# Gated recurrence and two MLPs on one core: attention of two blocks ahead of the first MLP, the two blocks taken in turns

## The chip, the cores and the metric

The kernel runs on one core of a Trainium2 chip. The metric is the device time of one launch in microseconds (us), lower being better. Three timed runs of the kernel before gave 1014.69, 1015.67 and 1017.27 us (median 1015.67); one more execution was taken with the hardware profiler and gave 1016.47 us.

## The reference

Three stages, one after the other. The first is a linear recurrence with a state of 48 x 48 for each of 4 batches and 8 heads over 768 steps; its output is laid out as 3072 tokens of 384 features. Then a SiLU MLP (384 to 2048 to 384) and a gated SiLU MLP (384 to 1536 to 384). All in float32.

```python
for t in range(S):                                   # B, H, S, D = 4, 8, 768, 48
    state = alpha[:, :, t, :, None] * state + np.einsum('bhd,bhe->bhde', k[:, :, t], v[:, :, t])
    y[:, :, t] = np.einsum('bhd,bhde->bhe', q[:, :, t], state)
x = y.transpose(0, 2, 1, 3).reshape(B * S, H * D)
h = x @ moe_w_in;  x1 = (h * sigmoid(h)) @ moe_w_out
g = x1 @ moe2_w_gate
out = ((g * sigmoid(g)) * (x1 @ moe2_w_val)) @ moe2_w_out
```

## The kernel before, in words

The recurrence is done in 24 chunks of 128 steps (6 per batch; chunk `n` is position `n // 4` of batch `n % 4`). A chunk has four head pairs, numbered `g = 4n + p`; two pairs make a duo `d`. For a duo, VectorE scans the decays (`stage_a1`, `stage_a3`), GpSimd multiplies k and q by them (`kq`, `stage_a2`, `stage_a3`). For a pair, TensorE forms the scores `s` (`qkt`), VectorE masks them into `pt` (`causal`), and ScalarE copies the transposed keys `kt` out of the same score tile (`keys`). For a chunk, TensorE then forms the output `y`, the state increment `ds` and, from chunk 4 on, the part of the old state (`pv`); `chunk_end` copies `y` into `x` (rounded on ScalarE, the remainder by a subtraction on VectorE) and updates the state. Head pair 0 of a chunk has to be spread over the unused rows of `x`: in the first block by extra matmuls (`spread`, `v3`), in later blocks by six DMAs from `y3` at the end of the block.

Matrix products are in float32 split into a rounded high part and a remainder, three matmuls for one. The scores of the chunks of the first block (`n < NE`) are plain float32 matmuls; later scores are split, which needs `stage_b` (ScalarE) and `stage_c` (VectorE, GpSimd) for each duo.

The first MLP takes the chunks in seven blocks of 4, 3, 3, 3, 3, 4 and 4 chunks; a step is one feature tile `f` of 16: `g1` (hidden `h`, nine matmuls), SiLU twice on ScalarE (`gh`, `gf`), a subtraction on VectorE (`gl`), `g2` (nine matmuls into three accumulators `x1`). While block `j` goes through its 32 half-steps (`slot`), the attention of block `j + 1` is issued pair by pair within 24 of them. The weights arrive as 64-bit words in 32 units (two for each feature); each unit takes three operations on VectorE (`decode_unit`, L47, L52, L57), one on ScalarE (`high_unit`) and one on GpSimd (`low_unit`); `units1` moves each of these stages one unit on. All 32 units are decoded while block 0 is in the MLP. The results of the first MLP go to DRAM, and the second MLP follows, in six blocks.

Each engine takes its instructions in program order, as this code emits them (a manual schedule): what stands ahead in an engine's queue holds up what stands behind. Loads go through SyncE's queue, which is in order as well; a chunk's input `in` has two buffers.

Of the kernel before, what the change touches and what calls it, by code (L numbers as in the profile page):

```python
# [20 lines left out]
DM = H * D  # L21
# [199 lines left out]
def fast(ctx, tc, pk, w1, w2, out, bad_i):  # L221
# [16 lines left out]
    wp = ctx.enter_context(tc.tile_pool(name="wp", bufs=2 * NF1))  # L238
    ps = ctx.enter_context(tc.tile_pool(name="ps", bufs=1, space=PSUM))
    mp = ctx.enter_context(tc.tile_pool(name="mp", bufs=2))  # L240

    def bank(i, name):
        return ps.tile([128, 512], F32, tag=f"b{i}", name=name)

# [25 lines left out]

    start = mp.tile([128, 6 * 512], F32, tag="big", name="start", bufs=3)
# [4 lines left out]
    in_t, v_t, r_t = {}, {}, {}  # L276
# [5 lines left out]
    def load_in(n):  # L282
        if n >= NCH:
            return
        t = ap.tile([128, A_W + 2 * W], F32, tag="in", name=f"in{n}")
        in_t[n] = t[:, :A_W], t[:, A_W:].rearrange("p (x r t) -> p x r t", x=2, r=NP)
        if n:
            SP.dma_start(out=t, in_=pk[n, :, :A_W + 2 * W])
            return
        for i in range(2):  # L290
            for lo, w in ((0, 2 * CA), (A_W, W // 2), (A_W + W, W // 2)):
                one = 0 if lo else 1
                cs = slice(lo + i * (w + one), lo + (i + 1) * w + one)
                SP.dma_start(out=t[:, cs], in_=pk[n, :, cs])

    def load_v(n):
# [86 lines left out]
    def qkt(g):  # L383

        d, i = divmod(g, 2)
        n, p = divmod(g, NP)
        kf, qf = kq_t[d][:, 0, i], kq_t[d][:, 1, i]
        if n < NE:

            b = [bank(k, f"s{g}_{k}") for k in ((0, 1), (5, 4))[g % 2]]  # L390
            for h in range(2):
                r = slice(64 * h, 64 * h + 64)
                PE.matmul(b[h][:, :C], kf[r], qf[r], start=True, stop=True)
            PE.matmul(b[0][:, C:C + 2 * D], kf, columns(ident), start=True, stop=True)
            s_t[g] = [x[:, :C] for x in b], b[0][:, C:C + 2 * D]
# [7 lines left out]
        s_t[g] = [b[:, :2 * C].rearrange("p (h t) -> p h t", h=2)], b[:, 2 * C:]  # L403

    def causal(g):
        if g < NE * NP and g % NP == 0:
            pt = p0[g // NP % 2]
        else:
            pt = ap.tile([128, 2, C], F32, tag="pt", name=f"pt{g}", bufs=NP + 1)
        pt_t[g] = pt  # L410
        s = s_t[g][0]
        if len(s) == 1:
            DVE.tensor_tensor(
                out=pt, in0=s[0],
                in1=mask.rearrange("p (o t) -> p o t", o=1).to_broadcast([128, 2, C]), op=ALU.mult,
            )
        else:
            for h in range(2):
                DVE.tensor_tensor(out=pt[:, h], in0=s[h], in1=mask, op=ALU.mult)

# [9 lines left out]
    def pv(n):  # L430
# [4 lines left out]
        v = v_t[n]  # L435
        early = n % 2 if n < NE else 0
        y = y_t[n] = bank((6, 2)[early], f"y{n}")
# [45 lines left out]
    def chunk_end(n):  # L483
# [3 lines left out]
        if i == 0:  # L487
            x_t[j] = mp.tile([128, 2, KT, 512], F32R, tag="big", name=f"x{j}", bufs=3)
            if j:
                y3_t[j] = mp.tile([128, 2, 512], F32R, tag="y3", name=f"y3_{j}", bufs=1)  # L490
# [77 lines left out]

    def g1(j, f, lo=0, hi=None):
        w = len(blocks1[j]) * C  # L570
        if (j, f) not in h_t:

            h_t[j, f] = bank(f % 2 + (6 if j == 0 and f < 2 else 0), f"h{j}_{f}")[:, :w]
        xk = [(x_t[j][:, 0, k, lo:hi or w], x_t[j][:, 1, k, lo:hi or w]) for k in range(KT)]
        product(h_t[j, f][:, lo:hi or w], unit_t["1", 2 * f], xk)

# [15 lines left out]
    def g2(j, f):  # L592
        w = len(blocks1[j]) * C
        if f == 0:
            x1_t[j] = [bank(2 + m, f"x1_{j}_{m}")[:, :w] for m in range(KT)]
        u = unit_t["1", 2 * f + 1]
        gh, gl = act_t.pop((j, f))
        for m in range(KT):
            PE.matmul(x1_t[j][m], part(u, m), gh, start=(f == 0), stop=False)  # L599
            PE.matmul(x1_t[j][m], part(u, m, 1), gh, start=False, stop=False)  # L600
        for m in range(KT):
            PE.matmul(x1_t[j][m], part(u, m), gl, start=False, stop=(f == NF1 - 1))  # L602
        if f == NF1 - 1:
            t0 = blocks1[j][0] * C
            ev = mp.tile([128, KT, 512], F32, tag="big", name=f"x1e{j}", bufs=3)
# [91 lines left out]
    def attn(lag=1, more=True, first=None):  # L697
# [9 lines left out]
        if new is not None:  # L707
            d, odd = divmod(new, 2)
            early = new < NE * NP
            ahead = d + (2 if early else 3)  # L710
            if early and new and not odd:
                up_to("a1", ahead, stage_a1, ND)
            causal(new)
            keys(new)
            if new == 0:
                up_to("a1", ahead, stage_a1, ND)
        if rest:
# [3 lines left out]
        if new is None:  # L721
            return
        if early and new % NP == 0:
            spread(new // NP)
        if odd:
            up_to("a3", ahead, stage_a3, ND)
            if not early:
                up_to("b", d + 2, stage_b, ND)
            up_to("gd", d, guard, ND)
        else:  # L730
            up_to("a1", ahead, stage_a1, ND)
            if not early:
                up_to("c", d + 1, stage_c, ND)
            up_to("a2", ahead, stage_a2, ND)

    late = []

    def load1(u):
# [3 lines left out]
        else:  # L742
            if u == NU1 - 4:
                late.append(mp.tile([128, 4, 2 * DM], I32, tag="big", name="late", bufs=3))
            load_unit(("1", u), w1_src(u), late[0][:, u - NU1 + 4])
# [34 lines left out]

    load_in(0)
    load_v(0)
    load_in(1)
    load_v(1)
# [23 lines left out]

    T0, BG, CG, TF, TE = 7, 2, 1, 1, 1

    first = NE * NP
    st["b"] = st["c"] = NE * NP // 2
    stage_a(0)
    stage_a(1)
    up_to("l1", 1, load1, NU1)
    for i in range(NP):
        ACT.activation(
            out=qh[:, i, 2 * C:].rearrange("p (h d) -> p h d", h=2), in_=columns(ident), func=AF.Copy
        )
    for g in range(first):  # L820
        attn(2)
        if g % 4 == 3:
            up_to("l1", g // 2 + 1, load1, NU1)
        if g >= T0:
            units1(0, 1 + (g - T0) // 2)
        if g == first - BG:
            up_to("b", first // 2, stage_b)
        if g == first - CG:
            up_to("c", first // 2, stage_c)

    for f in range(2):
        need1(2 * f)
        g1(0, f, 0, (NE - 1) * C)
        attn(1, False)
        for _ in range(TF):
            units1(8)
    up_to("b", first // 2 + 1, stage_b)
    stage_a(first // 2 + 2)
    for _ in range(TE):
        units1(8)  # L840

# [31 lines left out]

    steps = [(j, f) for j in range(NB1) for f in range(NF1)]
    def slot(j, hs, first=None):
        if j + 1 < NB1:
            done = sum(len(bl) for bl in blocks1[:j + 1]) * NP
            todo = len(blocks1[j + 1]) * NP
            due = sum(24 * m // todo <= hs for m in range(todo))
            attn(more=st["qk"] < done + due, first=first)  # L880
        else:
            attn(more=False, first=first)
        if j == 0:
            units1()

        if j == NB1 - 2 and hs == 26:
# [14 lines left out]

    g1(*steps[0], (NE - 1) * C)
    act1(*steps[0])()
    for s, (j, f) in enumerate(steps):
        need1(2 * f + 1)
        if s + 1 < len(steps):
            need1(2 * steps[s + 1][1])
            g1(*steps[s + 1], 0 if s else (NE - 1) * C)
        slot(j, 2 * f, (lambda: act1(*steps[s + 1])) if s + 1 < len(steps) else None)
        g2(j, f)  # L910
        slot(j, 2 * f + 1)

# [99 lines left out]
```

## Time and profile before

| | |
|---|---|
| timed runs, median of three | 1015.67 us |
| profiled execution | 1016.47 us |
| its span, first to last instruction | 1014.7 us |
| TensorE busy | 978.6 us (96%) |
| VectorE busy | 481.7 us (47%) |
| ScalarE busy | 366.3 us (36%) |
| GpSimd busy | 236.3 us (23%) |
| TensorE's mean granted clock | 0.979 of full speed |

The span falls into two parts. In the first 140 us TensorE is often idle or at half clock, and VectorE is busy most of the time. From 140 us to the end TensorE is busy without a break but for the last few microseconds. Attention of block 0 runs alone up to 43 us; the MLP of block 0, with all the weight decoding and the attention of block 1, from 43 to 154 us; the MLP of block 1, with the attention of block 2, from 154 to 218.5 us.

### The profile page before, as it was taken

What the parts mean: (1) busy time and instruction counts of PE and PEld (TensorE: products, weight loads), DVE (VectorE), ACT (ScalarE), POOL (GpSimd) and SP (SyncE); (2) the same over time, 40 slices, a digit from 0 to 9 for tenths busy, and PEclk for the clock granted to TensorE, in tenths of its full rate; (3) what the DMA queues carried; (4) which work ended last, traced back from release to release, by engine and by line L of the source; (5) the groups of instructions that cost most, each with busy time, mean ns of one, the idle gap of its engine ahead of it and who ended that gap; (6) DMA issues with size and microseconds to landing.
All of it is one profiled execution on the core that took longest, in us unless ns stands there. A gap on an engine that the chain in (4) does not pass through costs nothing.

```text
span 1014.7 us, 14287 instructions
## 1 busy us (share of the span) xinstructions
PE 978.6 (96%) x5600; PEld 865.1 (85%) x5600; DVE 481.7 (47%) x869; ACT 366.3 (36%) x874; POOL 236.3 (23%) x305
## 2 busy tenths in 40 slices
PE   7878889999999999999999999999999999999997
PEld 4666779999999999888788888888888888888886
DVE  5899974534445355352598755222222222222222
ACT  2344444544445455444354323222222222122121
POOL 4566662323223244230243211000000000000000
PEclk7799999999999999999999999999999999999999
DMA  6463322212222212200544420100100100100000
GB/s 203 148 249 96 139 82 73 74 52 77 55 66 74 77 56 89 71 14 3 187 149 131 156 63 16 63 1 1 63 0 1 63 1 1 63 1 11 22 1 35
DMA packets 27882, 69.08 MB, mean 68 GB/s; under 512 B 3104, under 2 KB 9248, under 8 KB 27808
## 3 DMA queue, kind: packets, MB, share of 16 engines
q1 hardware_dynamic: 27808, 68.10, 20.9%
q8 instruction: 46, 0.75, 0.3%
q14 instruction: 28, 0.23, 0.1%
HBM read 56.68 MB, written 9.44 MB: 65 GB/s over the span
## 4 chain that ended last, share of the span: by engine, by line
PE 86%; DVE 9%; issue 2%; DMA 1%; ACT 1%; SPq 0%; POOL 0%; ACTq 0%; DVEq 0%
PE gv L565 10%; PE gv L564 10%; PE gv L567 10%; PE h L564 6%; PE x L602 6%; PE x L600 5%; PE h L565 5%; PE x L599 5%; PE h L567 5%; PE o L669 5%; PE o L667 5%; PE o L668 5%; DVE raw L52 2%; PE y L445 2%; PE y L467 2%
## 5 line engine op out<-in xcount | busy, mean ns | idle before, releaser
L652 DVE TENSOR_TENSOR a<-gv,sg 128x512 f32<-128x512 f32 x72 | 49.7, 691 | 254.0 <-PE gv L567 254.0
L565 PE MATMUL gv<-x1h,w 128*128 128x512 f32 x432 | 169.1, 391 | 0.0
L564 PE MATMUL gv<-x1h,w 128*128 128x512 f32 x432 | 169.0, 391 | 0.0
L565 PE MATMUL h<-x,w 128*128 128x384 f32 (+2 forms) x342 | 123.7, 362 | 6.1 <-POOL w L250 6.1
L564 PE MATMUL h<-x,w 128*128 128x384 f32 (+2 forms) x342 | 125.3, 367 | 0.2 <-DVE x L250 0.2
L599 PE MATMUL x<-gh,w 128*128 128x384 f32 (+1 forms) x336 | 121.3, 361 | 2.7 <-ACT gh L583 2.6
L567 PE MATMUL gv<-x1l,w 128*128 128x512 f32 x432 | 122.1, 391 | 0.0
L600 PE MATMUL x<-gh,w 128*128 128x384 f32 (+1 forms) x336 | 121.2, 361 | 0.0
L250 DVE TENSOR_TENSOR gl<-gf,gh 128x384 fp32r<-128x384 f32 (+1 forms) x112 | 73.8, 659 | 75.9 <-ACT gf L584 74.1
L650 ACT ACTIVATE sg<-gv 128x512 f32<-128x512 f32 x72 | 43.0, 597 | 177.6 <-PE gv L567 177.6
L583 ACT ACTIVATE gh<-h 128x384 fp32r<-128x384 f32 (+1 forms) x112 | 59.7, 533 | 129.8 <-PE h L567 129.8
L250 POOL TENSOR_TENSOR w<-raw,w 128x384 fp32r<-128x384 f32 x64 | 77.5, 1218 | 108.2 <-ACT w L541 106.8
L253 ACT ACTIVATE ah<-a 128x512 fp32r<-128x512 f32 x72 | 45.5, 632 | 157.8 <-DVE a L652 157.8
L669 PE MATMUL o<-w,al 128*128 128x384 f32 x288 | 97.2, 338 | 0.0
L667 PE MATMUL o<-w,ah 128*128 128x384 f32 x288 | 97.0, 337 | 0.0
L668 PE MATMUL o<-w,ah 128*128 128x384 f32 x288 | 96.7, 336 | 0.0
L567 PEld LDWEIGHTS gv<-x1l,w 128*128 128x128 f32 x432 | 81.1, 188 | 17.8
L564 PEld LDWEIGHTS gv<-x1h,w 128*128 128x128 f32 x432 | 81.0, 188 | 15.2
L565 PEld LDWEIGHTS gv<-x1h,w 128*128 128x128 f32 x432 | 81.1, 188 | 14.9
L567 PE MATMUL h<-x,w 128*128 128x384 f32 (+2 forms) x342 | 86.8, 362 | 0.0
L602 PE MATMUL x<-gl,w 128*128 128x384 f32 (+1 forms) x336 | 84.5, 359 | 2.4 <-DVE gl L250 2.4
L565 PEld LDWEIGHTS h<-x,w 128*128 128x128 f32 x342 | 64.7, 189 | 13.1 <-POOL w L250 8.1
(105 smaller groups left out, 1581.3 us busy)
## 6 DMA issues: line engine op xcount, KB each, us to landing
raw<-in_w_dram SPq DMA_DIRECT2D x64, 384.0 KB, 4.9
in<-in_pk_dram SPq DMA_DIRECT2D x23, 770.5 KB, 4.3
in_v<-in_pk_dram SPq DMA_DIRECT2D x24, 256.0 KB, 3.3
x1r<-x_d SPq DMA_DIRECT2D x6, 768.0 KB, 5.4
out_dram<-ob SPq DMA_DIRECT2D x24, 192.0 KB, 2.1
x_d<-x1e SPq DMA_DIRECT2D x3, 768.0 KB, 4.6
x_d<-x1e SPq DMA_DIRECT2D x4, 576.0 KB, 3.3
late<-in_w_dram SPq DMA_DIRECT2D x4, 384.0 KB, 5.1
```

The costliest lines, as they stand in the source:

```text
L250: eng.tensor_tensor(out=lo, in0=src, in1=hi.bitcast(F32), op=ALU.subtract)
L564: PE.matmul(acc, part(u, k), xh, start=(k == 0), stop=False)
L565: PE.matmul(acc, part(u, k, 1), xh, start=False, stop=False)
L567: PE.matmul(acc, part(u, k), xl, start=False, stop=(k == len(xk) - 1))
L583: ACT.activation(out=gh, in_=hb, func=AF.Silu)
L599: PE.matmul(x1_t[j][m], part(u, m), gh, start=(f == 0), stop=False)
L600: PE.matmul(x1_t[j][m], part(u, m, 1), gh, start=False, stop=False)
L602: PE.matmul(x1_t[j][m], part(u, m), gl, start=False, stop=(f == NF1 - 1))
L652: DVE.tensor_tensor(out=a, in0=val, in1=sg, op=ALU.mult)
L667: PE.matmul(o, ah[:, ts], ohl[:, :DM], start=(f == 0), stop=False)
L668: PE.matmul(o, ah[:, ts], ohl[:, DM:], start=False, stop=False)
L669: PE.matmul(o, al[:, ts], ohl[:, :DM], start=False, stop=(f == NF2 - 1))
```

## The change

- Block 1's three chunks (4 to 6) are treated like block 0's: their 12 pairs are computed ahead of the first MLP, with plain float32 scores (`n < NF` = 7 in `qkt`), and without `stage_b` and `stage_c`. Weight decoding starts with the 17th pair (`T0 = first - 12`), at one unit for two pairs, the rate of before.
- The first MLP then takes blocks 0 and 1 in turns: features 0 and 1 of block 0, then two or three of block 1, one of block 0, and so on (`turns`), until block 1 has all 16 and block 0 has 8; then the other 8 of block 0, with the 12 pairs of block 2 in 10 half-steps. From block 2 on the order is as before.
- Block 1's accumulators use banks 5, 6 and 7, which attention leaves free meanwhile.
- The two score tiles of a pair become one tile over two banks, and one mask operation does both heads.
- The first loads are cut differently: chunk 0's k and q halves on two queues (q on ScalarE's), chunk 1 in five pieces ahead of v.
- The three large buffers `big` get fixed places, `spread` is called after a chunk's last pair.

```diff
-    NE = len(blocks1[0])
+    NE, NF = B, len(blocks1[0]) + len(blocks1[1])
@@ load_in
+        elif part == 2:
+            SP.dma_start(out=t[:, :A_W], in_=pk[n, :, :A_W])
+        else:
+            if n == 0:
+                cs = slice(part * (2 * CA + 1), (part + 1) * 2 * CA + 1)
                 SP.dma_start(out=t[:, cs], in_=pk[n, :, cs])
+            for x, eng in enumerate((SP, ACT) if n == 0 else (SP, SP)):
+                lo = A_W + x * W + part * (W // 2)
+                eng.dma_start(out=t[:, lo:lo + W // 2], in_=pk[n, :, lo:lo + W // 2])
@@ qkt
-        if n < NE:
+        if n < NF:
-            b = [bank(k, f"s{g}_{k}") for k in ((0, 1), (5, 4))[g % 2]]
+            b = pools_ps["early"].tile([128, 2, 512], F32, tag=f"s{g % 2}", name=f"s{g}")
@@ causal
-            for h in range(2):
-                DVE.tensor_tensor(out=pt[:, h], in0=s[h], in1=mask, op=ALU.mult)
+        DVE.tensor_tensor(
+            out=pt, in0=s_t[g][0],
+            in1=mask.rearrange("p (o t) -> p o t", o=1).to_broadcast([128, 2, C]), op=ALU.mult,
+        )
@@ the loads at the start
-    load_in(0)
+    load_in(0, 0)
+    load_in(0, 1)
+    load_in(1, 2)
+    load_in(1, 0)
     load_v(0)
-    load_in(1)
+    load_in(1, 1)
     load_v(1)
@@ the stage ahead of the MLP
+    T0 = first - 12
     for g in range(first):
         attn(2)
         if g % 4 == 3:
-            up_to("l1", g // 2 + 1, load1, NU1)
+            up_to("l1", g // 4 + 1, load1, NU1)
         if g >= T0:
-            units1(0, 1 + (g - T0) // 2)
+            units1(2, 1 + (g - T0) // 2)
...
+    FB = 8
+    turns = [(0, 0), (0, 1)]
+    for k, n in enumerate((2, 2, 2, 2, 3, 3, 2)):
+        f1 = sum(j for j, _ in turns)
+        turns += [(1, f1 + i) for i in range(n)] + [(0, k + 2)] * (k + 2 < FB)
+    steps = turns + [(0, f) for f in range(FB, NF1)]
+    steps += [(j, f) for j in range(2, NB1) for f in range(NF1)]
@@ slot
-        if j == 0:
+        if s < len(turns) and (j == 0 or half == 0):
             units1()
@@ the steps
+    need1(0)
+    g1(0)
+    attn(1, False)
     act1(*steps[0])()
```

VectorE's queue after the last score of a chunk, in the stage ahead of the MLP. Before, chunk 2: `x` is the remainder of the chunk's output, `g` and `r` the scans, `start` and `pt` masked scores, `raw` and `dec` the weights.

```order
L250 TENSOR_TENSOR x_280<-y_442,x_280 128x3x128
L337 SCALAR_TENSOR_TENSOR g_478<-in_316,rc_86 128x258
L47 TENSOR_SCALAR dec_3_485<-raw_3_319 128x384
L318 SCALAR_TENSOR_TENSOR r_492<-in_316,ones 128x258
L419 TENSOR_TENSOR pt_494<-s_0_487,mask 128x128
L419 TENSOR_TENSOR pt_494<-s_1_488,mask 128x128
```

Now, chunk 4, the first of block 1's:

```order
L261 TENSOR_TENSOR x_605<-y_572,x_605 128x3x128
L261 TENSOR_TENSOR y_1_606<-y_572,y_1_606 128x128
L521 TENSOR_TENSOR state_95<-ds_581,state_95 128x192
L357 SCALAR_TENSOR_TENSOR g_614<-in_461,rc_89 128x258
L52 SCALAR_TENSOR_TENSOR raw_2_308<-raw_2_308,dec_2_570 128x384
L57 SCALAR_TENSOR_TENSOR raw_2_308<-raw_2_308 128x384
L338 SCALAR_TENSOR_TENSOR r_626<-in_461,ones 128x258
L431 TENSOR_TENSOR pt_628<-s_622,mask 128x256
```

Between the chunk's remainder and the mask there stand two more operations for block 1's chunks (`y`, `state`), and two decoding operations in place of one; the mask is one operation.

VectorE's queue in the MLP. Before, one feature of block 0 (from one `gl` up to the next), with attention of block 1 between (`r`, `ql`, `pt`):

```order
L250 TENSOR_TENSOR gl_2_716<-gf_2_715,gh_2_714 128x512
L337 SCALAR_TENSOR_TENSOR g_723<-in_414,rc_87 128x258
L52 SCALAR_TENSOR_TENSOR raw_9_578<-raw_9_578,dec_9_697 128x384
L47 TENSOR_SCALAR dec_10_738<-raw_10_580 128x384
L57 SCALAR_TENSOR_TENSOR raw_9_578<-raw_9_578 128x384
L52 SCALAR_TENSOR_TENSOR raw_10_580<-raw_10_580,dec_10_738 128x384
L47 TENSOR_SCALAR dec_11_754<-raw_11_582 128x384
L57 SCALAR_TENSOR_TENSOR raw_10_580<-raw_10_580 128x384
L413 TENSOR_TENSOR pt_776<-s_767,mask 128x256
L250 TENSOR_TENSOR gl_3_773<-gf_3_772,gh_3_771 128x512
```

Now, from feature 2 of block 0 (512 columns) over features 2 and 3 of block 1 (384 columns):

```order
L261 TENSOR_TENSOR gl_2_931<-gf_2_930,gh_2_929 128x512
L52 SCALAR_TENSOR_TENSOR raw_10_819<-raw_10_819,dec_10_902 128x384
L47 TENSOR_SCALAR dec_11_939<-raw_11_838 128x384
L57 SCALAR_TENSOR_TENSOR raw_10_819<-raw_10_819 128x384
L261 TENSOR_TENSOR gl_2_965<-gf_2_964,gh_2_963 128x384
L52 SCALAR_TENSOR_TENSOR raw_11_838<-raw_11_838,dec_11_939 128x384
L47 TENSOR_SCALAR dec_12_973<-raw_12_862 128x384
L57 SCALAR_TENSOR_TENSOR raw_11_838<-raw_11_838 128x384
L52 SCALAR_TENSOR_TENSOR raw_12_862<-raw_12_862,dec_12_973 128x384
L47 TENSOR_SCALAR dec_13_991<-raw_13_880 128x384
L57 SCALAR_TENSOR_TENSOR raw_12_862<-raw_12_862 128x384
L261 TENSOR_TENSOR gl_3_1008<-gf_3_1007,gh_3_1006 128x384
```

The scans and masks are gone from between the `gl`; what is left is decoding and the `gl` of two blocks.

TensorE's queue at the entry to the MLP as it is now: `s_725` is the last early score, `y_750` the output of chunk 6, `x_605` block 1's input, which chunk 6 completes.

```order
L414 MATMUL s_725<-start,kq_631 128x96
L579 MATMUL h_0_740<-x_272,w_0_533 128x512
...
L482 MATMUL y_750<-kq_631,state_97 48x128 x4
L579 MATMUL h_1_795<-x_272,w_2_634 128x512
...
L617 MATMUL x_0_2_823<-gl_0_791,w_1_568 128x512
L579 MATMUL h_0_840<-x_605,w_0_533 128x384
```

Before, block 0's second and further features stood where `h_0_840` stands now, and block 1's first product came only after block 0's last feature.

## Rows read from the trace of the kernel before

**Rows 1.** Busy time by stretch: us, then PE, PEld, DVE, ACT, POOL, clock, DMA.

```profile
43.20:140.00 96.80, 78.52 (x468) 63.01 (x469) 93.48 (x151) 45.81 (x120) 64.40 (x66) 0.93 0.44 153
140.00:1014.70 874.70, 867.40 (x4906) 778.00 (x4904) 358.88 (x646) 307.66 (x711) 151.80 (x201) 1.00 0.17 53
```

**Rows 2.** VectorE, the start: the scan of chunk 1.

```profile
11.67 0.70 DVE L318 TENSOR_TENSOR_SCAN r<-in,ones 128x258 f32<-128x258 f32 x1 [3.07 <-DMA in<-in_pk_dram]
```

**Rows 3.** TensorE in order of time, attention of chunks 0 and 1: start, duration.

```profile
16.34 0.70 PE L445 MATMUL y<-pt,in_v 128*64 128x128 f32 x4
...
19.98 0.49 PE L393 MATMUL s<-kq 64*128 64x128 f32 x4
...
20.79 0.49 PE L393 MATMUL s<-kq 64*128 64x128 f32 x4
...
24.33 0.80 PE L393 MATMUL s<-kq 64*128 64x128 f32 x4 [1.84 <-POOL kq L342]
...
25.73 0.70 PE L445 MATMUL y<-pt,in_v 128*64 128x128 f32 x4
```

**Rows 4.** TensorE, matmuls of block 0 behind a wait of 1.21 us.

```profile
72.90 0.50 PE L565 MATMUL h<-x,w 128*128 128x512 f32 x1 [1.21 <-POOL w L250]
73.23 0.39 PE L564 MATMUL h<-x,w 128*128 128x512 f32 x1
```

**Rows 5.** VectorE, a unit decoded while GpSimd idles, and the end of chunk 4.

```profile
53.08 0.55 DVE L52 SCALAR_TENSOR_TENSOR raw<-raw,dec 128x384 int32<-128x384 int32 x1
...
54.40 0.69 DVE L318 TENSOR_TENSOR_SCAN r<-in,ones 128x258 f32<-128x258 f32 x1
...
85.27 0.56 DVE L250 TENSOR_TENSOR x<-y,x 128x384 fp32r<-128x384 f32 x1 [1.00 <-ACT x L493]
...
86.73 0.65 DVE L52 SCALAR_TENSOR_TENSOR raw<-raw,dec 128x384 int32<-128x384 int32 x1
```

**Rows 6.** TensorE in order of time, steady steps and the end of block 1.

```profile
143.07 0.39 PE L564 MATMUL h<-x,w 128*128 128x512 f32 x1
...
147.15 0.39 PE L564 MATMUL h<-x,w 128*128 128x512 f32 x1
...
201.24 0.32 PE L400 MATMUL s<-qh,kh 128*128 128x352 f32 x1
...
201.68 0.33 PE L599 MATMUL x<-gh,w 128*128 128x384 f32 x1
...
203.36 1.09 PE L445 MATMUL y<-pt,in_v 128*64 128x128 f32 x16
...
205.84 0.45 PE L564 MATMUL h<-x,w 128*128 128x384 f32 x1
...
209.10 0.33 PE L564 MATMUL h<-x,w 128*128 128x384 f32 x1
...
212.22 0.33 PE L564 MATMUL h<-x,w 128*128 128x384 f32 x1
...
218.46 0.33 PE L564 MATMUL h<-x,w 128*128 128x384 f32 x1
```

**Rows 7.** The six DMAs that spread pair 0 of block 1, and such DMAs' landing.

```profile
141.28 3.97 SPq L514 DMA_DIRECT2D x<-y  x6
...
x<-y SPq DMA_DIRECT2D x24, 48.0 KB, 2.1
```

**Rows 8.** Groups of VectorE and GpSimd, 81 to 137 us: count, busy us, mean ns.

```profile
L57 DVE SCALAR_TENSOR_TENSOR raw<-raw 128x384 int32<-128x384 int32 x15 | 13.8, 921 | 0.0
L52 DVE SCALAR_TENSOR_TENSOR raw<-raw,dec 128x384 int32<-128x384 int32 x15 | 12.7, 845 | 0.0
L47 DVE TENSOR_SCALAR dec<-raw 128x384 int32<-128x384 int32 x14 | 9.9, 705 | 0.5
L250 DVE TENSOR_TENSOR gl<-gf,gh 128x512 fp32r<-128x512 f32 x9 | 6.5, 724 | 0.0
...
L250 POOL TENSOR_TENSOR w<-raw,w 128x384 fp32r<-128x384 f32 x16 | 19.7, 1250 | 0.0
```

More of the change, by code (lines that the diff above doesn't have):

```diff
@@ L268, in fast @@
     kts = [ac.tile([128, 2, 64], F32, name=f"kt{i}") for i in range(NP + 1)]
-    start = mp.tile([128, 6 * 512], F32, tag="big", name="start", bufs=3)
+    start = big(0, "start")
     ident = start[:, :C]
@@ L567, in product, with g1 @@
             PE.matmul(acc, part(u, k), xl, start=False, stop=(k == len(xk) - 1))
-    def g1(j, f, lo=0, hi=None):
+    def g1(s):
+        j, f = steps[s]
         w = len(blocks1[j]) * C
[L571 to L575, printed above, removed]
+        h_t[j, f] = bank(s % 2, f"h{j}_{f}")[:, :w]
+        xk = [(x_t[j][:, 0, k, :w], x_t[j][:, 1, k, :w]) for k in range(KT)]
+        product(h_t[j, f], unit_t["1", 2 * f], xk)
     def act1(j, f):
@@ L594, in g2 @@
         if f == 0:
-            x1_t[j] = [bank(2 + m, f"x1_{j}_{m}")[:, :w] for m in range(KT)]
+            x1_t[j] = [bank((5 if j == 1 else 2) + m, f"x1_{j}_{m}")[:, :w] for m in range(KT)]
         u = unit_t["1", 2 * f + 1]
@@ L715, in attn @@
             if new == 0:
-                up_to("a1", ahead, stage_a1, ND)
+                up_to("a1", ahead, stage_a1, top)
         if rest:
@@ L722, in attn @@
             return
-        if early and new % NP == 0:
+        if new < NE * NP and new % NP == NP - 1:
             spread(new // NP)
         if odd:
-            up_to("a3", ahead, stage_a3, ND)
+            up_to("a3", ahead, stage_a3, top)
             if not early:
@@ L822, in fast @@
         if g % 4 == 3:
-            up_to("l1", g // 2 + 1, load1, NU1)
+            up_to("l1", g // 4 + 1, load1, NU1)
         if g >= T0:
-            units1(0, 1 + (g - T0) // 2)
[L826 to L840, printed above, removed]
+            units1(2, 1 + (g - T0) // 2)
+    pe_stack.close()
+    pools_ps["late"] = ctx.enter_context(tc.tile_pool(name="ps_l", bufs=1, space=PSUM))
+    FB = 8
[5 more added lines that the diff above has]
+    steps += [(j, f) for j in range(2, NB1) for f in range(NF1)]
+    due, n = [first] * (2 * len(turns)), first
+    for j, slots, over in [(2, 2 * (NF1 - FB), 10)] + [(j, 2 * NF1, 24) for j in range(3, NB1)]:
+        todo = len(blocks1[j]) * NP
+        due += [n + sum(over * m // todo <= i for m in range(todo)) for i in range(slots)]
+        n += todo
+    due += [NG] * (2 * NF1)
     def start_phase2():
@@ L872, in flag, with slot @@
         DVE.tensor_copy(bad_i, fb[:, 0:1])
[L874 to L882, printed above, removed]
-        if j == 0:
-            units1()
+    def slot(s, half, first=None):
+        j, f = steps[s]
+        hs = 2 * f + half
+        target = due[2 * s + half]
+        attn(more=st["qk"] < target, first=first)
+        if st["qk"] < target:
+            attn()
+        if s < len(turns) and (j == 0 or half == 0):
+            units1()
+        ahead = 2 * (len(turns) - s) - half
+        if ahead == 6:
+            stage_a(first_d)
+        if ahead == 4:
+            stage_a(first_d + 1)
+            up_to("b", first_d, stage_b)
+        if ahead == 2:
+            up_to("c", first_d, stage_c)
+        if ahead == 1:
+            stage_a(first_d + 2)
+            up_to("b", first_d + 1, stage_b)
         if j == NB1 - 2 and hs == 26:
@@ L900, in slot @@
                 prep_x1(0, (hs - 6) // 2)
-    g1(*steps[0], (NE - 1) * C)
+    first_d = first // 2
+    need1(0)
+    g1(0)
+    attn(1, False)
     act1(*steps[0])()
```

73 lines of the change are left out of this document (35 added, 38 removed).

## The prediction

> **What bounds the kernel now.** I read the busy times by stretch first. From 140 us to the end TensorE is busy for 867.4 of 874.7 us at full clock [rows 1]; nothing on another engine can shorten that part, and the change leaves its matmuls as they are. From 43.2 to 140 us TensorE is busy for 78.5 of 96.8 us at a mean clock of 0.93, while VectorE is busy for 93.5, 97% of the stretch [rows 1]: there VectorE sets the pace, with the decoding of the weights, the subtractions `gl` and block 1's attention in one queue. So the question is how early TensorE comes into its unbroken stretch. I then read TensorE in order of time to find a point at which both kernels have done the same work: block 0 and block 1 through the first MLP, the attention of chunks 0 to 9, and the first product of block 2. Before, that is at 218.5 us, where block 2's second product starts [rows 6]; what follows is the same in both. The forecast is that moment in the changed kernel: the length of the attention stage, plus TensorE's work from there on at full clock, plus what it waits.
>
> **The attention stage.** Seven chunks run ahead of the first product, in place of four.
> - Start. Before, VectorE has masked the first scores at 8.60 and then waits 3.07 us for chunk 1's input, until 11.67 [rows 2]; the first output matmul of chunk 0 follows 4.67 us later, at 16.34 [rows 3]. Now chunk 1's decays are issued as a piece of their own ahead of v. No row shows such a piece, nor loads on ScalarE's queue. At best the decays are there at 8.60 and the output starts at 13.3; with no gain at 16.3; a loss beyond that I put at 0.5, for pieces that delay each other. I take the good end, since the piece is a third of the bytes and stands two loads earlier, and 0.5 less because TensorE's waits become short: after a wait of 1.21 us its matmuls still took 0.39 [rows 4], the time of the steady stretch [rows 6], whereas after 1.84 us a score matmul took 0.80 in place of 0.49 [rows 3]. So 12.8.
> - Chunks 0 to 2. From output to output it took 9.39 us [rows 3], a chain: output 3.64 (16.34 to 19.98), a score 0.81, mask, ScalarE's copy, remainder, scan, GpSimd's product, then a score at half clock (24.33 to 25.73). This chain is unchanged. The merged mask does not shorten it: it removes an instruction for each of 28 pairs, but the copy of the keys now follows the mask of both heads. I cost it at zero, with bounds of 0.1 us each way for a chunk. The first of the three cycles has its output at full clock, 1.3 less. Together 8.05 + 2 x 9.39 = 26.8.
> - Chunk 3. Weight decoding begins. Between the scan and the mask that frees the score tile there stand two decoding operations and a scan. A unit of three took 1.32 us with GpSimd idle [rows 5] and 2.47 by the contended means, 921 + 845 + 705 ns [rows 8]; two of the three, a scan of 0.7 and the mask, in place of the 1.1 us of GpSimd's product, add 1.5 to 2.3. I take 1.9: 11.3.
> - Chunk 4. Two more operations stand behind the remainder, which with ScalarE's copy between took 1.46 us before the next (85.27 to 86.73) in place of about 0.47: 1.0 more. The output has the state's part and not the spreading: 2.48 us at full clock [rows 6], 3.7 to 5.0 at lower clock, I take 4.4, 0.8 more. So 13.1.
> - Chunk 5 up to the first product, which needs the score tile of the last pair but one: the same chain without the two scans and the last score, 10.2 (9 to 11).
>
> Sum 12.8 + 26.8 + 11.3 + 13.1 + 10.2 = 74.2 us; with the bounds 71 to 80. Before, the first product came at 43.2, the end of the first stretch [rows 1]. Plain scores take 0.81 us a pair (19.98 to 20.79) against 0.44 split (201.24 to 201.68), 4.4 us more for 12 pairs, but they are inside this chain, where TensorE waits anyway, and six duos lose their splitting on three engines.
>
> **TensorE's work from there to the common point,** from the steady rows [rows 6]: a step of 512 columns 4.08 us (143.07 to 147.15), one of 384 columns 3.12 (209.10 to 212.22), a pair of split scores 0.44, an output 2.48 (203.36 to 205.84). Chunk 6's output 2.5, 16 x 4.08 = 65.3, 16 x 3.12 = 49.9, block 2's first product 1.6, 12 x 0.44 = 5.3, three outputs 7.4: 132.0 us.
>
> **What TensorE waits in that stretch.**
> - The first product and part of chunk 6's output run at half clock, since TensorE has idled for about 3 us before: 2.5 more (0 to 4). SiLU of the first product stands behind chunk 6's copies on ScalarE: 0.3.
> - Block 1's input. Its pair 0 is spread by six DMAs, issued in 3.97 us and landing 2.1 us after issue [rows 7]. Before, block 0's last steps hid this. Now block 1's first product is the third: behind chunk 6's output stand only block 0's second product and first `g2`, 4.1 us and the 0.3. The DMAs can start some 2.0 us after the output, when the copies are done; the fourth, which the first matmul needs, lands at 6.1 and the sixth at 7.4. Between a wait of 1.7 and one of 3.0 I take 2.4, and 1.0 for the clock that falls in it.
> - The turns. A turn of one step of block 0 and two of block 1 is 4.08 + 2 x 3.12 = 10.3 us on TensorE; VectorE must do four units in it and three `gl`. GpSimd then has one operation of 1.25 us for each unit [rows 8], 48% of the time, against 64.4 of 96.8 us, 67%, before [rows 1]. Between 1.32 us (GpSimd idle) and 2.47 (contended) that gives, in proportion, 2.15 for a unit. With 0.72 for a wide `gl` and an estimated 0.6 for each narrow one (between three quarters of that and the same), VectorE needs 8.6 + 1.9 = 10.5 us: level with TensorE. A `gl` is due some 4.2 us after its product and takes 1.9 with the SiLU ahead, so 2.3 us of lateness costs nothing; four turns late by 0.2 stay inside it. I take 1.0.
> - Block 2's attention in 10 half-steps, not 24: 1.5 (0 to 5), for the scans' latency and for its six DMAs, which have three half-steps to land.
>
> Sum 8.7.
>
> **A rule against it.** A unit's decoding took 1.32 us with GpSimd idle [rows 5] and 2.47 with GpSimd at work for two thirds of the time [rows 8]; so the two engines slow each other, and a stretch in which GpSimd works less decodes faster. The Trainium skill, page "SBUF — State Buffer", section "Who interferes with whom", says that a VectorE instruction with two SBUF inputs contends with a GpSimd instruction that reads SBUF, and that of the two the later one is blocked wholly until the other ends. By that rule, one GpSimd operation of 1.25 us would cost VectorE up to 1.25 us for each unit, 2.57 in all, and a turn of 12.2 us, close to the first rival below. The trace agrees that there is contention; what it costs here no row shows, and the sum does without the rule.
>
> **The sum.** 74.2 + 132.0 + 8.7 = 214.9 us against 218.5: 3.6 us earlier, and the rest is unchanged. The profiled execution took 1016.47 us (span 1014.7 and 1.8 around it), so this one would take 1012.9; it was 0.8 above the median of 1015.67, and against that median the forecast is 1012.1.
>
> **Rivals.**
> - VectorE becomes the bound of the turns: a unit costs 2.47, as in the contended stretch [rows 8]. A turn then takes VectorE 9.9 + 1.9 = 11.8 us against 10.3, and the two turns with three steps of block 1 (13.4 on TensorE; five units, four `gl`) 14.9: 1.5 late six times, 9.0, less the 2.3 of slack and the 1.0 counted: 5.7 more, and about 1 for TensorE's clock that falls in the waits. 1018.8, slower. It decides from a unit of 2.2 on, where lateness of six turns outgrows the slack. For it: VectorE's 97% [rows 1]. Against: GpSimd has no attention in the turns.
> - The start brings nothing: chunk 1's decays land at 11.7 as now. 3.5 more, 1015.6, no change. For it: the same bytes go through the same engines; against: v and half of k and q no longer stand ahead of them.
> - The waits hide: no half clock at the entry (2.5), the six DMAs seen only by 1, the turns and block 2 free (2.5), chunks 3 to 5 at the low end (1.5). About 1004 to 1006.
> - The change doesn't do what it says: the blocks are not taken in turns because block 1's input is late. The order of the queues is fixed by the code, so only the wait above is left of this.
>
> **Chances.** Forecast 0.42, VectorE bound 0.24, no gain at the start 0.18, waits hidden 0.16. A measurement of this kernel can tell about 0.3%, 3 us, from no change; the forecast lies just beyond that, so a little over half of it counts as faster (0.25), with the last rival (0.16) and a part of the others (0.04): 0.45. Slower is the first rival, and the low odds that entry and start both fail: 0.25. Within 0.3%: 0.30. The likeliest case by itself runs from 1008 to 1016 (the attention stage 71 to 77); the range takes in the hidden waits and the VectorE bound: 1004 to 1020.
>
> **What would show it.** First product at 74 us, chunk 0's output at 12.8, no wait for DMA at the second scan: the attention stage is right. One wait of 2 to 3 us for the DMA of `x` ahead of block 1's first product. In the turns TensorE above 95%, VectorE near 95%, units at 2.1 to 2.2 us; if instead TensorE waits for `gl` at each turn, the first rival holds. Block 2's second product at 215 us, and from there 796 us as before. The forecast is wrong if the first product comes after 80 us, or if TensorE idles for more than 10 us between the entry and 215 us.

## The result and the profile after

The changed kernel takes 1024.64 us (median of 4 runs, 1024.31 to 1025.6) against 1016.47 for the kernel before (4 runs): ratio 1.0085, 95% interval 1.0070 to 1.0099. It is 8.2 us slower; 1012.1 was forecast, with a range up to 1020.

The windows of the changed kernel, in the columns of [rows 1]: the attention stage, the entry to the MLP, the turns, block 2's attention, and the rest behind the common point (the start of block 2's second product, up to which both kernels have done the same work).

```profile
0.00:79.95 79.95, 58.73 (x437) 45.57 (x437) 48.44 (x105) 23.86 (x86) 36.08 (x59) 0.71 0.46 155
79.95:98.77 18.82, 16.98 (x93) 12.88 (x94) 8.10 (x14) 5.33 (x14) 3.36 (x3) 0.80 0.37 110
98.77:170.86 72.09, 72.09 (x380) 67.37 (x379) 63.84 (x97) 32.78 (x69) 30.07 (x29) 1.00 0.31 111
170.86:227.09 56.23, 52.70 (x343) 42.83 (x343) 32.14 (x64) 27.84 (x80) 27.96 (x40) 0.97 0.28 87
227.09:1023.90 796.81, 789.03 (x4370) 703.35 (x4368) 323.49 (x571) 270.90 (x610) 125.33 (x164) 1.00 0.17 52
```

The same of the kernel before, around the stretch shown in [rows 1]:

```profile
0.00:43.20 43.20, 32.64 (x229) 24.07 (x229) 29.31 (x75) 12.87 (x45) 20.13 (x39) 0.72 0.55 187
...
140.00:218.46 78.46, 78.46 (x537) 74.65 (x536) 35.66 (x75) 37.35 (x102) 26.72 (x37) 1.00 0.20 60
```

The rest is as long as before (796.8 us, and 1014.7 - 218.46 = 796.2 [rows 6]). All of the loss lies ahead of the common point: 227.09 against 218.46. Up to there TensorE is idle for less time than before: 227.09 less the four busy times is 26.6 us, before 218.46 - 189.6 = 28.8. It is its busy time that grew, from 189.6 to 200.5 us. Of these 10.9 us, 4.4 are the plain scores of block 1's 12 pairs (0.81 us for 0.44 a pair, [rows 3] and [rows 6]). The clock column points to the rest: 80 us at 0.71 of full speed, where before it was 43.2 us at 0.72.

TensorE, chunks 0 and 1 (beside [rows 3]), and VectorE's scan of chunk 1 (beside [rows 2]):

```profile
14.16 0.70 PE L460 MATMUL y<-pt,in_v 128*64 128x128 f32 x4
...
17.80 0.80 PE L413 MATMUL s<-kq 64*128 64x128 f32 x4
...
19.20 0.49 PE L413 MATMUL s<-kq 64*128 64x128 f32 x4
...
23.01 0.80 PE L413 MATMUL s<-kq 64*128 64x128 f32 x4 [2.06 <-ACT kt L440]
...
24.41 0.70 PE L460 MATMUL y<-pt,in_v 128*64 128x128 f32 x4
```

```profile
8.98 1.07 DVE L338 TENSOR_TENSOR_SCAN r<-in,ones 128x258 f32<-128x258 f32 x1
```

The scan waits no more, and the output starts 2.2 us earlier. The cycle from output to output is 10.25 us, not 9.39, and the 0.86 more has two parts. The output takes 3.64 as before, but the first score behind it takes 1.40 in place of 0.81 (half clock: a score matmul group of 0.80, not 0.49): 0.59. From the second score of the cycle to the fourth it takes 3.81 (19.20 to 23.01) in place of 3.54 (20.79 to 24.33 in [rows 3]), since the fourth now waits for ScalarE's copy of the keys instead of GpSimd's product: 0.27. The output starts of all seven chunks are 14.16, 24.41, 34.65, 44.90, 56.87, 69.43 and 84.08.

The entry to the MLP, and block 2's first scores (beside [rows 6]):

```profile
79.95 0.79 PE L579 MATMUL h<-x,w 128*128 128x512 f32 x1 [3.45 <-ACT kt L440]
...
84.08 1.09 PE L460 MATMUL y<-pt,in_v 128*64 128x128 f32 x16
86.56 0.50 PE L579 MATMUL h<-x,w 128*128 128x512 f32 x1
...
92.93 0.41 PE L579 MATMUL h<-x,w 128*128 128x384 f32 x1 [1.78 <-DMA x<-y]
...
176.60 0.32 PE L420 MATMUL s<-qh,kh 128*128 128x352 f32 x1
...
179.37 0.50 PE L420 MATMUL s<-qh,kh 128*128 128x352 f32 x1 [2.17 <-ACT kt L440]
...
180.18 0.63 PE L614 MATMUL x<-gh,w 128*128 128x512 f32 x1
```

The first product runs at half clock behind its wait (79.95 to 84.08, 4.1 us for a full-clock 2.05), and block 1's first product waits for the spreading DMAs. At 176.60 two pairs stand in one half-step: the second waits 2.17 us for the one score tile, and the product after it is at half clock (matmuls of 0.63 us, not 0.39). On VectorE the first pair's mask stands behind two scans meanwhile, and ScalarE's copy follows the mask:

```profile
176.66 0.68 DVE L338 TENSOR_TENSOR_SCAN r<-in,ones 128x258 f32<-128x258 f32 x1
...
177.57 1.14 DVE L357 TENSOR_TENSOR_SCAN g<-in,rc 128x258 f32<-128x258 f32 x1
178.64 0.39 DVE L431 TENSOR_TENSOR pt<-s,mask 128x256 f32<-128x256 f32 x1
```

### The profile page after: what moved, and what is told of

The parts are those of the page before. It is cut to its first block, busy times and chain, and to the rows that moved or that the text cites. A ratio compares the mean times of both kernels' runs of the same rounds, so it can differ in the third digit from the quotient of the medians.

```text
span 1023.9 us, 14306 instructions
## 1 busy us (share of the span) xinstructions
PE 989.5 (97%) x5618; PEld 872.0 (85%) x5618; DVE 476.0 (46%) x847; ACT 360.7 (35%) x856; POOL 222.8 (22%) x293
## 4 chain that ended last, share of the span: by engine, by line
PE 91%; DVE 4%; ACT 2%; DMA 1%; issue 1%; SPq 0%; ACTq 0%; DVEq 0%
PE gv L580 10%; PE gv L579 10%; PE gv L582 10%; PE h L579 7%; PE h L580 6%; PE h L582 6%; PE x L615 6%; PE x L614 6%; PE x L617 6%; PE o L684 5%; PE o L682 5%; PE o L683 5%; PE y L460 3%; PE y L482 2%; PE ds L474 1%; PE s L420 1%
## 5 line engine op out<-in xcount | busy, mean ns | idle before, releaser
L579 PE MATMUL h<-x,w 128*128 128x384 f32 (+1 forms) x336 | 124.0, 369 | 5.3 <-ACT kt L440 3.4
L580 PE MATMUL h<-x,w 128*128 128x384 f32 (+1 forms) x336 | 121.8, 362 | 0.0
L261 POOL TENSOR_TENSOR w<-raw,w 128x384 fp32r<-128x384 f32 x64 | 75.0, 1172 | 162.7 <-ACT w L556 159.9
L582 PE MATMUL h<-x,w 128*128 128x384 f32 (+1 forms) x336 | 85.4, 362 | 0.0
```

What stands on the lines that cost most here:

```text
L261: eng.tensor_tensor(out=lo, in0=src, in1=hi.bitcast(F32), op=ALU.subtract)
L579: PE.matmul(acc, part(u, k), xh, start=(k == 0), stop=False)
L580: PE.matmul(acc, part(u, k, 1), xh, start=False, stop=False)
L582: PE.matmul(acc, part(u, k), xl, start=False, stop=(k == len(xk) - 1))
```

## The experiments

The table has milestones of each kernel's one profiled execution (us), and the times. "First" is block 0's first product, "common" block 2's second. Each ratio is to runs of the kernel before on the same chip, whose medians lie between 1015.70 and 1016.88 us.

| kernel | chunk 0 out | first | common | median us | ratio to before [95%] |
|---|---|---|---|---|---|
| before | 16.34 | 43.16 | 218.46 | 1016.47 | |
| changed | 14.16 | 79.95 | 227.09 | 1024.64 | 1.0085 [1.0070, 1.0099] |
| changed again | 14.15 | 79.73 | 227.00 | 1025.05 | 1.0090 [1.0073, 1.0107] |
| two masks | 13.52 | 75.86 | 223.26 | 1022.96 | 1.0059 [1.0036, 1.0083] |
| dense covered | 14.11 | 78.63 | 223.01 | 1020.33 | 1.0043 [1.0028, 1.0058] |
| entry three | 13.79 | 78.25 | 221.04 | 1018.63 | 1.0016 [1.0000, 1.0033] |
| decode gap | 13.95 | 75.30 | 219.66 | 1016.52 | 1.0003 [0.9989, 1.0017] |
| fillers | 15.30 | 69.15 | 214.55 | 1012.58 | 0.9956 [0.9937, 0.9974] |
| loads alone (on before) | 13.78 | 40.79 | 216.12 | 1014.46 | 0.9975 [0.9965, 0.9985] |
| loads, fill (on before) | 14.96 | 38.71 | 213.88 | 1011.94 | 0.9964 [0.9949, 0.9979] |
| all four | 13.68 | 71.93 | 210.03 | 1009.45 | 0.9928 [0.9902, 0.9954] |
| all five | 15.35 | 70.11 | 208.18 | 1006.66 | 0.9903 [0.9881, 0.9926] |
| one each | 13.29 | 62.39 | 200.48 | 1003.84 | 0.9885 [0.9868, 0.9901] |

**Changed again.** 

> The changed kernel once more, nothing edited. The same instructions gave 78.3 and 78.6 us for the first product in two runs whose edits come later in the program, and 79.95 in the first profile. Theory A (the granted clock falls differently from one execution to the next, by a microsecond or two of the attention stage): first product between 78 and 80, 1022 to 1025. Rival B (79.95 was an outlier and with it much of the loss): 1018 to 1020.

The first product came at 79.73 and the time was 1025.05: the loss is no outlier. The same instructions gave 78.25 and 78.63 for the first product on another chip (entry three and dense covered, whose edits come later in the program).

**Fillers.**

```diff
+            if new < NF * NP and new % NP == NP - 1:      # behind qkt(new)
+                for _ in range(5 if new < NE * NP else 9):
+                    PE.matmul(fill_t[new], mask, mask3, start=True, stop=True)   # unused columns of s
```

> The changed kernel, but in the attention stage five (nine from chunk 4 on) bfloat16 matmuls of 384 columns, whose results nothing reads, stand behind the fourth score of each chunk, where TensorE waits 2 to 4.6 us. Theory A (the half clock of scores and outputs, which follows those waits, is on the chain): outputs fall from 3.6 to 2.3 us and first scores from 1.4 to 0.8, a cycle of chunks 0 to 2 to about 8.2, the first product comes near 70 us, and its own half clock goes too; 1012 to 1015. Rival B (the clock does not rise for so little, and the added matmuls stand in the way of the next score): first product at 80 or later, 1025.

From 20 to 40 us, the changed kernel, and with fillers:

```profile
20.00:40.00 20.00, 15.88 (x127) 13.26 (x126) 9.61 (x22) 5.60 (x22) 7.75 (x10) 0.66 0.39 138
```

```profile
20.00:40.00 20.00, 15.78 (x163) 11.75 (x165) 14.19 (x33) 8.14 (x32) 11.03 (x15) 1.00 0.45 154
```

TensorE is busy for the same time, but the granted clock is 1.00 in place of 0.66. TensorE in order of time with fillers (`s<-mask` are the fillers):

```profile
20.62 0.98 PE L726 MATMUL s<-mask 128*128 128x384 bf16 x5
22.84 0.49 PE L416 MATMUL s<-kq 64*128 64x128 f32 x4 [1.25 <-ACT kt L444]
...
23.66 0.55 PE L464 MATMUL y<-pt,in_v 128*64 128x128 f32 x3
...
25.79 0.49 PE L416 MATMUL s<-kq 64*128 64x128 f32 x4
```

With 0.98 us of the wait filled, the output takes 2.13 us (23.66 to 25.79), not 3.64, and the cycles are 8.36, 7.57 and 7.56 where they were 10.25. The first product comes at 69.15, and the whole is 12 us faster. Theory A holds: half clock was on the chain of the attention stage. No other single edit gave as much; the next, decode gap, gave 8.

**Two masks.**

```diff
-            b = pools_ps["early"].tile([128, 2, 512], F32, tag=f"s{g % 2}", name=f"s{g}")
+            b = [pools_ps["early"].tile([128, 512], F32, tag=f"s{g % 2}_{k}", name=f"s{g}_{k}") for k in range(2)]
@@ causal
+            for h in range(2):
+                DVE.tensor_tensor(out=pt[:, h], in0=s[h], in1=mask, op=ALU.mult)
```

> The changed kernel, but with the two score tiles of one bank and the two mask operations of a pair that the kernel before had. Theory A (the copy of the keys waits for the one mask over both banks, and the next chunk's first score waits for that copy): the cycles of chunks 0 to 2, from output to output, fall from 10.25 to about 10.0 us, the later ones by as much, the first product comes at 78.4 in place of 79.95 us, the time falls by 1.5 to 1023.1. Rival B (the merged mask is neutral; a cycle is longer than the 9.39 of before only because its first score now runs at half clock, 0.6 us): cycles of 10.2, first product at 79.9, 1024.6.

The time was 1022.96, as theory A has it (1023.1), but the trace gives it only a part. What TensorE's scores wait for, changed kernel, then with two masks (total, times, longest):

```profile
PE s L413 <- ACT kt L440: 14.8, 6, 4.6
...
PE s L413 <- POOL kq L362: 1.0, 1, 1.0
```

```profile
PE s L413 <- ACT kt L445: 9.1, 4, 4.4
PE s L413 <- POOL kq L362: 6.5, 4, 1.8
```

The keys' copy no longer ends the wait; GpSimd's product does, as in [rows 3]. What that brings can be read apart from the clock, from the second score of a cycle to the fourth. With two masks:

```profile
17.22 0.49 PE L413 MATMUL s<-kq 64*128 64x128 f32 x4
...
20.77 0.49 PE L413 MATMUL s<-kq 64*128 64x128 f32 x4 [1.85 <-POOL kq L362]
```

That is 3.55 us, and as much in the next two cycles; the kernel before has 3.54. With the merged mask it is 3.81 in all three cycles of the changed kernel, and in those of dense covered and entry three. So the merged mask with its one tile over two banks costs 0.26 us a chunk. The cycles were 8.06, 9.62 and 9.89. The first had part of its output at full clock; all four, with the same two masks, had that too (8.12), loads alone, also with two masks, had not (9.51), so what brings it stays open. The intervals of this kernel and of the changed one overlap; how much of the 1.7 us between their medians is the mask's stays open.

**Decode gap.**

```diff
-        if g >= T0:
-            units1(2, 1 + (g - T0) // 2)
+        if g >= T0 and g % NP == 0:
+            for i in range(4):
+                units1(2, 2 * (g - T0) // NP + 1 + i // 2)
```

> The changed kernel, but with the six units that are decoded in the attention stage issued two at a time behind the first mask of chunks 4, 5 and 6, where VectorE has nothing to do for 4.5 us while the output runs; the chain from remainder to mask has no decoding in it any more. Theory A (the decoding operations are on the chain, 1.5, 1.4 and 1.1 us of it in chunks 3, 4 and 5): the cycles fall from 11.97, 12.56 and 10.52 to 10.5, 11.1 and 9.5 us, the first product comes 4 us earlier, the time is 1020.6. Rival B (two units at the contended price take 4.9 us and now hold up the first mask behind the output): cycles as they are, 1024.6.

The first product in this kernel:

```profile
75.30 0.50 PE L579 MATMUL h<-x,w 128*128 128x512 f32 x1 [2.11 <-ACT kt L440]
```

The cycles of chunks 3 to 5 (the last one up to the first product) became 10.38, 11.70 and 8.69; they were 11.97, 12.56 and 10.52. That is 4.3 less: theory A. The time fell by 8, twice as much. Behind the shorter wait (2.11 in place of 3.45 us) most of the first product is at full clock: it takes 2.9 in place of 4.1. Block 1's first product takes 2.2 in place of 2.9, and block 0's second `g2` behind it 2.1 in place of 2.9.

**Entry three.**

```diff
-    turns = [(0, 0), (0, 1)]
+    turns = [(0, 0), (0, 1), (0, 2)]
...
-        turns += [(1, f1 + i) for i in range(n)] + [(0, k + 2)] * (k + 2 < FB)
+        turns += [(1, f1 + i) for i in range(n)] + [(0, k + 3)] * (k + 3 < FB)
```

> The changed kernel, but with three features of block 0 ahead of block 1's first product in place of two. Theory A (block 1's first product waits for the six DMAs that spread its pair 0, and the half clock of what follows comes from that wait): the wait of 1.78 us and the half clock of the two products after it go, 3 to 4 us; 1021. Rival B (the entry runs at half clock because TensorE did little in the attention stage, and units for feature 2 are not decoded in time): a wait for w takes the place of the one for x, 1024.6.

Block 0's third product and block 1's first, in this kernel:

```profile
89.26 0.39 PE L579 MATMUL h<-x,w 128*128 128x512 f32 x1
...
93.34 0.33 PE L579 MATMUL h<-x,w 128*128 128x384 f32 x1
```

There is no wait, and both are at full clock. From the first product to the common point it takes 142.79 us, where the changed kernel takes 147.14: 4.35 less, theory A. The rest of the 6 us is the attention stage of this execution, 1.7 shorter.

**Dense covered.**

```diff
+    due[lo:lo + 10] = [first + m for m in (1, 2, 3, 4, 6, 7, 8, 10, 11, 12)]   # lo = 2 * len(turns)
@@ slot
+        two = target - st["qk"] == 2
-        attn(more=st["qk"] < target, first=first)
+        attn(99 if two else 1, more=st["qk"] < target, first=first)   # score, then output, then score
```

> The changed kernel, but with block 2's 12 pairs placed otherwise in the same 10 half-steps: where a half-step takes two pairs, one stands ahead of the chunk's output and one behind it, so that no score stands right behind another one. Theory A (two pairs in one half-step wait for the single score tile, because the mask and the copy of the keys stand behind scans on VectorE): the waits of 2.17 and 1.22 us and the half clock after the first, 1.7, go; from 170.9 us to block 2's second product it takes 51 in place of 56.2 us; the time is 1019.6. Rival B (twelve pairs in ten half-steps are too many for the chain of scans, GpSimd's products and the splitting, wherever they stand): the waits come back at other scores, 1024.

The waits for the score tile, changed kernel and this one:

```profile
PE s L420 <- ACT kt L440: 3.4, 2, 2.2
```

```profile
PE s L420 <- ACT kt L440: 1.2, 4, 0.5
```

Both long waits and the half clock are gone, but the stretch is shorter by only 2.75 us, not 5: four short waits and gaps of some 0.3 us at other scores came in, which is what rival B said. So each theory is right by half. That the time fell by 4.3 is in part the attention stage of this execution, 1.3 shorter.

**Loads alone, and with fillers, on the kernel before.**

`load_in` is that of the change; the calls, each line of the code in one here:

```diff
-    load_in(0); load_v(0); load_in(1); load_v(1)
+    load_in(0, 0); load_in(0, 1); load_in(1, 2); load_in(1, 0); load_v(0); load_in(1, 1); load_v(1)
```

> The kernel before with nothing changed but the cutting and order of the first loads. Theory A (the start is a chain that everything behind hangs on): output of chunk 0 at 14.2 in place of 16.3 us, first product at 41.1 in place of 43.2, the time 2 us shorter, 1014.4. Rival B (VectorE, 97% busy from 43 to 140 us, sets the pace there and is not earlier): first product at 41.1, but block 0 ends when it did, 1016.4.

The stretch from first product on, against [rows 1]:

```profile
40.79:137.70 96.91, 78.60 (x468) 63.12 (x469) 93.68 (x151) 45.87 (x120) 64.45 (x66) 0.93 0.44 153
```

The time was 1014.46: theory A. VectorE's stretch is as long as before and starts 2.4 us earlier, so the whole gain of the start stays. This part of the change was good.

> The kernel before with the new first loads and five filling matmuls behind the fourth score of each of its four early chunks; nothing reads what these write. Theory A (half clock is on the chain of the attention stage of this kernel too): three cycles of 9.5 fall to about 8.2, first product at 37 in place of 41 us; VectorE, which sets the pace from there on, starts its queue earlier as well: 1011.5. Rival B (the clock does not rise, or VectorE's queue ends when it did): 1014.5.

The time was 1011.94, near theory A's number. The cycles were 7.56, 8.92 and 9.09, since the clock was full in only part of the stage: it was 0.50 from 30.04 to 36.40 us, behind the fillers of 27.20 us and the wait that they left.

```profile
30.04 0.80 PE L404 MATMUL s<-kq 64*128 64x128 f32 x4 [1.87 <-ACT kt L437]
```

**All four, all five.** The edits are those above together.

> The changed kernel with four edits together: two mask operations and score tiles of one bank; two pairs of block 2 around an output; three features of block 0 ahead of block 1; decoding behind the first mask of a chunk. Theory A (the four costs are separate places on one path): their gains of about 2, 2.8, 4.4 and 4 us add up to 13; 1011.5. Rival B (VectorE sets the pace of the turns once they begin earlier, since the units do not come earlier there): half of it, 1018.

The time was 1009.45, 15.2 us under the changed kernel: near theory A. The medians of the four single runs had fallen by 20.1 together, which is more, in part because the attention stage was shorter by 1.3 and 1.7 us in dense covered and entry three, whose edits don't touch it.

> The changed kernel with the four edits together (two mask operations, pairs around an output, three features of block 0 first, decoding behind the first mask) and the filling matmuls, whose results nothing reads. Theory A (the half clock of the attention stage is a cost of its own beside the four places): in the run with fillers alone a cycle of chunks 0 to 2 fell from 10.25 to 7.56 us; with the decoding off the chain chunks 3 to 5 come to about 8.5, 9.3 and 7.5, the first product near 65 us in place of 71.9, the time is 1002.5. Rival B (with the decoding moved, the waits in which the fillers stand are shorter, and the nine fillers of chunks 4 to 6 now hold up the next score): first product at 69 or later, 1007 to 1009.

The time was 1006.66, with the first product at 70.11: rival B. VectorE, then TensorE, at the masks of chunk 4:

```profile
47.30 0.27 DVE L438 TENSOR_TENSOR pt<-s,mask 128x128 f32<-128x128 f32 x1
48.75 0.29 DVE L438 TENSOR_TENSOR pt<-s,mask 128x128 f32<-128x128 f32 x1 [1.18 <-PE s L731]
```

```profile
44.74 0.52 PE L416 MATMUL s<-kq 64*128 64x128 f32 x4 [1.47 <-ACT kt L449]
...
45.72 3.00 PE L731 MATMUL s<-mask 128*128 128x384 bf16 x9
```

The nine fillers took 3.00 us, at a granted clock of 0.53, and the mask of the same tile's second bank waited for them. In the run with fillers alone nine took 1.63 us at 1.00.

**One each.**

Against all five:

```diff
-                for _ in range(5 if new < NE * NP else 9):
+                for _ in range(5 if new < NE * NP else 5):
...
-        if g >= T0 and g % NP == 0:
-            for i in range(4):
-                units1(2, 2 * (g - T0) // NP + 1 + i // 2)
+        if g >= NP and g % NP == 0:
+            for i in range(2):
+                units1(2, g // NP)
```

> As the version with all five edits, but one unit is decoded behind the first mask of each chunk from chunk 1 on, in place of two from chunk 4 on, and five filling matmuls stand in every chunk, in place of five and nine. Theory A (with the output at full clock the gap on VectorE is some 3 us, so one unit of 1.3 to 2.3 us fits and two, 4 us, do not; nine fillers at half clock, 3.0 us, hold up the next mask): chunk 3 to 5 cycles of 8, 8.8 and 7.5 us, TensorE at full clock from 20 us on, first product near 63 us, 1000. Rival B (the decoding now stands in the gaps of chunks 0 to 2 too and makes these cycles longer than 7.5): first product at 67 or later, 1004.

Up to its first product, and the entry:

```profile
0.00:62.39 62.39, 49.55 (x472) 35.29 (x472) 51.13 (x134) 23.99 (x86) 38.18 (x59) 0.97 0.60 199
62.39:80.00 17.61, 17.61 (x116) 14.62 (x117) 10.03 (x17) 6.89 (x18) 3.29 (x3) 1.00 0.44 141
```

The clock is 0.97 in place of 0.71, and there is no idle time at the entry. The cycles are 7.8, 8.0, 8.0, 8.2, 9.2 and 7.9, and the first product is near theory A's 63. The first three are longer than the 7.4 to 7.6 of fillers and all five by some 0.4, so rival B is right in part. This profiled execution took 1000.76 us; the other three took 1003.78 to 1004.51, so its milestones are those of the best of four. The median of 1003.84 us, 1.15% under the kernel before, is the fastest version. Loads and fillers alone bring the kernel before to 0.9964 of its time, one each to 0.9885, so some 8 us remain for the new order of work as it is here. The idea of the change is sound; its arrangement cost more than it brought.

## Why the prediction was wrong

It missed the common point by 227.09 - 214.9 = 12.2 us. By its own terms:

- Start: the first output came at 14.16 us for 12.8, inside its bounds; +1.4.
- **Chunks 0 to 2, the first failed step:** they took 30.74 us for 26.8, +3.9. I carried over a cycle of 9.39 whose first score was at full clock, and gave one output to full clock because TensorE's waits at the start became shorter. But the waits of 2 us in each cycle stayed, and with them half clock on every output and every first score. The output of the first cycle is 1.3 of the 3.9, three first scores are 1.8, and the merged mask, costed at zero with 0.1 us each way, is three times 0.26, 0.8. The fillers took these three cycles to 23.49, so half clock was 7.3 us of the 30.74. The kernel before had shown that 9.39 was no rule: its next cycle (25.73 to 36.22) took 10.49, with one decoding operation in it and with its first score at half clock.

```profile
29.37 0.80 PE L393 MATMUL s<-kq 64*128 64x128 f32 x4
...
30.52 0.49 PE L393 MATMUL s<-kq 64*128 64x128 f32 x4
...
36.22 0.70 PE L445 MATMUL y<-pt,in_v 128*64 128x128 f32 x4
```

- Chunks 3 to 5 and the first product: 11.97 + 12.56 + 10.52 = 35.05 for 34.6. Decode gap shows the mechanism: decoding was on the chain. But here too half clock was taken for granted, not seen as something to be bought back.
- Entry: 18.82 us hold 12.2 of work at full clock (two products and two `g2` of 512 columns, one product of 384, one output, by [rows 6]), a loss of 6.6; 6.2 was forecast. Both causes are confirmed: the half clock of the first product by fillers, where it took 2.28 us in place of 4.13, and the DMAs by entry three.
- Turns: they took 72.09 us without a wait, a loss of 0.8 against full rates; 1.0 was forecast.
- **Block 2's attention in 10 half-steps, the second failed step and the larger:** 56.23 us hold 8 x 4.08 + 2 x 1.56 + 12 x 0.44 + 3 x 2.48 = 48.5 of work, so 7.7 lost; I took 1.5, with a bound of 5. I thought of the chain's latency and not of the score tile, which has one buffer: two pairs in a half-step stand one right behind the other, and the second waits for mask and copy, which stand behind scans. The two waits (3.4) and the half clock after the first (1.7) are 5.1 of the 7.7; dense covered took both away and still lost 5.0 there, so nearly half of what they cost came back at other scores.

The sum, 1.4 + 3.9 + 0.4 + 0.4 - 0.2 + 6.2, is the 12.2 within rounding.

The first rival had the sign and not the mechanism. VectorE's groups in the turns (count, busy us, mean ns):

```profile
L57 DVE SCALAR_TENSOR_TENSOR raw<-raw 128x384 int32<-128x384 int32 x21 | 15.8, 751 | 0.0
L52 DVE SCALAR_TENSOR_TENSOR raw<-raw,dec 128x384 int32<-128x384 int32 x20 | 15.2, 758 | 0.0
L47 DVE TENSOR_SCALAR dec<-raw 128x384 int32<-128x384 int32 x20 | 15.0, 751 | 0.7
L261 DVE TENSOR_TENSOR gl<-gf,gh 128x384 fp32r<-128x384 f32 x15 | 8.3, 552 | 3.7 <-ACT gf L598 3.4
```

By these means a unit cost 2.26 us, above the 2.2 from which I let that rival decide, and TensorE still never waited: VectorE was busy for 63.84 of 72.09 us and itself waited for SiLU. The durations overlap a little, though, and the 1.32 us with GpSimd idle was read from start to start; read so, a unit in the turns took 2.17 on average, near the 2.15 of the prediction and below that rival's 2.2. The sum over the whole stretch decides, not the sum of the dearest turn.

The rule of the Trainium skill ("SBUF — State Buffer", "Who interferes with whom") says that the later of the two instructions is blocked until the other ends. The trace agrees. The 2.57 us for a unit, with which the prediction bounded that cost from above, were not reached. Here is one unit on VectorE, then GpSimd:

```profile
110.75 0.55 DVE L52 SCALAR_TENSOR_TENSOR raw<-raw,dec 128x384 int32<-128x384 int32 x1
111.33 0.36 DVE L47 TENSOR_SCALAR dec<-raw 128x384 int32<-128x384 int32 x1
111.61 1.40 DVE L57 SCALAR_TENSOR_TENSOR raw<-raw 128x384 int32<-128x384 int32 x1
```

```profile
111.50 1.09 POOL L261 TENSOR_TENSOR w<-raw,w 128x384 fp32r<-128x384 f32 x1 [1.35 <-ACT w L556]
```

GpSimd's operation ends at 112.59 and VectorE's third, which takes 0.55 in the unit before, at 113.01. In the turns each unit has one such long operation (1.27 to 1.40 for 0.55, or 1.07 for 0.36), and the unit shown takes 2.18 us from start to start, 0.86 more than with GpSimd idle.

"No gain at the start" is refuted by loads alone, "waits hidden" by the entry.

## What to carry to other kernels

Before work is moved into a stage of its own, ask at which clock TensorE runs there: this stage cost 80 us at 0.71, and a few matmuls in its idle time gave back 10.8 of them, 12 in the whole. Durations taken from rows of a stage hold only with the clock these rows had, so write the clock beside each. Where steps are packed closer, look for the resource with one buffer between them, and put independent work between its two uses; here that gave back a third of what was lost.

## What the runs showed of the hardware

- Five bfloat16 matmuls of 384 columns, 0.98 us in a wait of 2.2, kept the granted clock of 20 to 40 us at 1.00 (2.4 GHz) where it was 0.66 without them. They are not free: at a clock of 0.53 nine of them took 3.00 us and held up a mask.
- The gain depends on the wait that is left. In the kernel before, with loads and fillers, 1.04 us were left behind one chunk's fillers and the next score was at full clock (0.49); behind the next chunk's, 1.87 us were left, the score took 0.80, and the clock was 0.50 from 30.04 to 36.40 us. Up to the first product it was 0.82.
- GpSimd's operation on the weights holds up VectorE's decoding: one of a unit's three operations ended only behind it (at 113.01 and 112.59 us) and took 1.40 us in place of 0.55.
- The same instructions of the attention stage took from 78.25 to 79.95 us up to the first product, in four executions; the cycles of chunks 0 to 2 ran from 9.66 to 10.25.
